# A fused FFT mixing and MoE kernel: the scheduler's order replaced by one from a list scheduler with measured lengths

## The chip, the cores and the metric

The kernel runs on one core of a Trainium2 chip. Its time is the device time of one execution in microseconds (us). Five engines each work through a queue of their own in order: TensorE (PE, with its weight loads shown as PEld), VectorE (DVE), ScalarE (ACT), GpSimd (POOL) and SyncE (SP), which only issues DMAs. They meet at semaphores: an instruction waits at the head of its queue until what it reads is written and what it overwrites has been read.

## The reference

Eight sequences of 3136 positions and 256 channels go through a real FFT along the positions, a complex 256 x 256 mixing, a soft threshold, the inverse FFT, and then one SoLU feed-forward layer for each of the 25088 tokens:

```python
X = np.fft.rfft(x, axis=1)                       # x: (8, 3136, 256)
Yr = Xr @ w_r - Xi @ w_i + b_r;  Yi = Xr @ w_i + Xi @ w_r + b_i
Y = sign(Y) * max(abs(Y) - 0.01, 0)              # on Yr and Yi
y = np.fft.irfft(Yr + 1j * Yi, n=3136, axis=1)
h = y.reshape(25088, 256) @ w_in                 # (25088, 1024)
solu = h * softmax(h)
ln = (solu - mean(solu)) / sqrt(var(solu) + 1e-6) * g_ln
out = ln @ w_out                                 # (25088, 256)
```

## The kernel before

Nearly all matmuls are in fp16 with every operand split into a high and a low half, so a product takes three matmuls (high by high, high by low, low by high).

**Front, for each of the 8 batches b.** The FFT of 3136 = 98 x 32 goes in two steps. `load_peak` (L190) loads x in 8 pieces and takes their largest value; `set_scales` (L200) makes powers of two of it. `fwd1` (L238) loads x again in 8 chunks, splits it (xh, xl), multiplies by the 98-point matrix (L254) and writes s1 to DRAM; batch 0 uses `fwd1_first` in f32 (L261) and takes its peaks on the way. `fwd2` (L313) is the 32-point step in 13 units (12 of two frequencies, one of one): it loads `bin` from s1, multiplies (L337) and splits into Xh and Xl. `mix` (L395, with L385, for batch 0 L363) is the complex mixing and the threshold. `inv1` (L416, L438) is the inverse 32-point step, in two halves of PE's rows, and writes s2 to DRAM. `inv2` (L462, L473) loads `zt` from s2 in 8 groups, does the inverse 98-point step, and writes 392 tokens at a time, transposed, to a ring of 1024 tokens (`ring_hi`, `ring_lo`).

**Feed-forward, for each of 196 tiles of 128 tokens.** `moe_head` (L493): 2 x 6 matmuls of 512 columns (L504) into PSUM tiles `ph` (3 buffers), the row's maximum (L507), a handful of one-column operations, the exponential (L524) and its product with h (L525) into `u` (4 buffers). `moe_turn` (L536): u split into `lh` (L540, ScalarE) and `ll` (L542, GpSimd), each transposed by a DMA of SyncE (L545) into `th` and `tl` (3 buffers each), and the variance (L549 to L553). `moe_tail` (L556): 24 matmuls of 256 columns (L563) into the one buffer of `po`, the scaled copy (L566) and the stores (L574). Weights come as 64-bit floats and are turned into f32 on VectorE and GpSimd by `load_wide` (L148).

**What sets the order.** The program is written in an order by hand: front units of batch b + 1, with the loads and fwd1 of batch b + 2 beside them, are handed out between the tiles of batch b by shares of their estimated cost (`front_b`, `with_shares`, `advance`, L724 to L758). A head is followed by its turn two tiles later, and that by its tail two tiles later; inv2 runs up to two tiles ahead of need (L780). The framework's scheduler then sets each engine's order, going by this program order and by a simulation of the engines' times (`schedule_with_timeline_sim=True`, L817). A few loads are held back by a tiny GpSimd copy into their buffer that reads an earlier load (L153, L180, L196):

```python
nc.gpsimd.tensor_copy(t[:1, 0, 0, :1], before)
nc.sync.dma_start(t, src)
```

Of the kernel before, what the change touches and what calls it, by code (L numbers as in the profile page):

```python
# [94 lines left out]

@with_exitstack
def fft_mix_solu_kernel(ctx: ExitStack, tc, x, w_r, w_i, b_r, b_i, w_in, w_out, g_ln, fa, fa16, fb, fs, gb, gs, ia, out):
    nc = tc.nc
    B, _, D = x.shape
    FF = w_in.shape[1]  # L100
    P = 128
# [8 lines left out]
    const = ctx.enter_context(tc.tile_pool(name="const", bufs=1))  # L110
    dram = ctx.enter_context(tc.tile_pool(name="dram", bufs=2, space=DRAM))
    xp = ctx.enter_context(tc.tile_pool(name="xp", bufs=2))
    fp = ctx.enter_context(tc.tile_pool(name="fp", bufs=2))
    mp = ctx.enter_context(tc.tile_pool(name="mp", bufs=2))
    sp = ctx.enter_context(tc.tile_pool(name="sp", bufs=4))
    ps_h = ctx.enter_context(tc.tile_pool(name="ps_h", bufs=3, space=PSUM))
    ps_o = ctx.enter_context(tc.tile_pool(name="ps_o", bufs=1, space=PSUM))
    ps_f = ctx.enter_context(tc.tile_pool(name="ps_f", bufs=4, space=PSUM))
# [25 lines left out]
    make_identity(nc, ident)  # L144
# [3 lines left out]
    def load_wide(dst, src, before=None):  # L148
# [3 lines left out]
        if before is not None:  # L152
            nc.gpsimd.tensor_copy(raw[:1, :1].bitcast(F32), before)  # L153
# [24 lines left out]
    def load_after(t, src, before):  # L178

        nc.gpsimd.tensor_copy(t[:1, 0, 0, :1], before)  # L180
        nc.sync.dma_start(t, src)
# [8 lines left out]
    def load_peak(b, c):  # L190

        n = S * D // P // NPK
        t = xp.tile([P, C1], F32, name="xt", bufs=3)[:, :n]
        if b == 1 and c < 3:

            nc.gpsimd.tensor_copy(t[:1, :1], raw[0, 4][:1, 0, :1])  # L196
        nc.sync.dma_start(t, x[b].rearrange("s d -> (s d)").rearrange("(p c n) -> c p n", p=P, c=NPK)[c])
        note_peak(b, c, NPK, t)
# [39 lines left out]
    def fwd1(b, c):  # L238
# [11 lines left out]
        for h in range(C1 // HF):  # L250
            hs = slice(h * HF, (h + 1) * HF)
            pa = front_psum(b)
            for i, (t, j) in enumerate(((xh, 0), (xh, 1), (xl, 0))):
                nc.tensor.matmul(pa[:N1], fa16_s[:, j], t[:, hs], start=i == 0, stop=i == 2)  # L254
# [6 lines left out]
    def fwd1_first(c):  # L261
# [9 lines left out]
        for h in range(C1 // HF):  # L271
            hs = slice(h * HF, (h + 1) * HF)
            pa = front_psum(0)
            nc.tensor.matmul(pa[:N1], fa_s, xt[:, hs], start=True, stop=True)
            nc.scalar.copy(av[:, hs], pa[:N1])
# [9 lines left out]
    def load_bin(b, g):  # L285
# [8 lines left out]
        nc.sync.dma_start(t, v[:, g * QG : (g + 1) * QG])  # L294
        raw[b, g] = t
        load_after(gb_s[g].rearrange("p u r t m -> p u (r t) m"), gb[:, g * QG // 2 : (g + 1) * QG // 2].rearrange("p u r t m -> p u (r t) m"), t[:1, 0, :1])
        if g + 1 < Q // QG:
            load_after(fb_s[g + 1], fb[:, (g + 1) * QG : (g + 2) * QG], t[:1, 0, :1])
# [14 lines left out]
    def fwd2(b, u):  # L313
# [11 lines left out]
        else:  # L325
# [3 lines left out]
            bt, fw = bins[b, g], [fb_s[g][:, gi + i] for i in range(2)]  # L329

        pb = front_psum(b)
        pv = pb.rearrange("p (r h i c) -> p r h i c", r=2, h=ND, i=2)
        for i in range(n):
            for dh in range(ND):
                ds = slice(dh * P, (dh + 1) * P)
                for k, (t, j) in enumerate(((0, 0), (0, 1), (1, 0))):
                    nc.tensor.matmul(pv[:, :, dh, i], bt[:, gi + i, t, ds], fw[i][:, j], start=k == 0, stop=k == 2)  # L337

        xh = fp.tile([P, 3, ND, 2, 2 * N2], F16, name="Xh16", bufs=2)
        xl = fp.tile([P, 3, ND, 2, 2 * N2], F16, name="Xl", bufs=2)  # L340
        if b:
            xs = fp.tile([P, ND, 2, 2 * N2], F32, name="Xs", bufs=1)
            nc.scalar.activation(xs[:, :, :n], pv[:, 1, :, :n], AF.Copy, scale=B_SCALE)
# [9 lines left out]
    def mix_first(u):  # L353
# [3 lines left out]
        xh, xl = Xs.pop((0, u))  # L357
        pm = front_psum(0)
        k = 0
        for part in (1, 0):  # L360
            for dh in range(ND):
                for x, w in ((xh, w_hi), (xh, w_lo), (xl, w_hi)):
                    nc.tensor.matmul(  # L363
                        pm[:M], x[:, part, dh, :n], w[dh][:, 1 - part : 3 - part], start=k == 0, stop=k == 6 * ND - 1
                    )
                    k += 1
        t = fp.tile([P, 2, D], F32, name="yt")
# [5 lines left out]
    def mix_split(b, u):  # L373
# [6 lines left out]
        ps, pm = front_psum(b), front_psum(b)  # L380
        for part, wp, out in ((2, 1, ps[:M, :D]), (1, 4, pm[:M, :D]), (0, 3, pm[:M, D:])):
            k = 0
            for dh in range(ND):
                for x, w in ((xh, w_hi), (xh, w_lo), (xl, w_hi)):
                    nc.tensor.matmul(out, x[:, part, dh, :n], w[dh][:, wp], start=k == 0, stop=k == 3 * ND - 1)  # L385
                    k += 1
        t = fp.tile([P, 2, D], F32, name="yt")
# [28 lines left out]
    def inv1(b, u0, u1):  # L416
# [14 lines left out]
        for u in range(u0, u1):  # L431
            yh, yl = Ys.pop((b, u))
            for k, (t, j) in enumerate(((yh, 0), (yl, 0), (yh, 1))):
                for ri in range(2):
                    for i in range(n):
                        rows = slice(i * half, (i + 1) * half)
                        gw = gs_s[:, ri, j] if n == 1 else gb_s[g][rows, u % 2, ri, j]
                        nc.tensor.matmul(  # L438
                            pz[i][:K, (u - u0) * D : (u - u0 + 1) * D], gw, t[rows, ri], start=k + ri == 0, stop=k + ri == 3
                        )  # L440
# [21 lines left out]
    def inv2(b, g):  # L462
# [5 lines left out]
        for eh in range(ND):  # L468
            pa = ps_f.tile([P, HF], F32, name="pf")
            for i in range(G2):  # L470
                es = slice(eh * P, (eh + 1) * P)
                for k, (t, j) in enumerate(((0, 0), (0, 1), (1, 2))):
                    nc.tensor.matmul(pa[:, i * N1 : (i + 1) * N1], zt[:, i, t, es], ia_s[:, j], start=k == 0, stop=k == 2)  # L473
# [19 lines left out]
    def moe_head(k, spare):  # L493
# [4 lines left out]
        for h in range(2):  # L498
# [3 lines left out]
            for dh in range(ND):  # L502
                for lh, rh in ((hi, win_hi), (hi, win_lo), (lo, win_low)):
                    nc.tensor.matmul(p, lh[:, dh], rh[:, dh, cs], start=n == 0, stop=n == 3 * ND - 1)  # L504
                    n += 1
# [50 lines left out]
    def moe_tail(k, parts, r, spare=False):  # L556
# [3 lines left out]
        for part, halves in ((th, 2), (tl, 1)):  # L560
            for f in range(NF):
                for j in range(halves):
                    nc.tensor.matmul(po[:, :D], part[:, f], wout[:, f, j], start=n == 0, stop=n == 3 * NF - 1)  # L563
                    n += 1
# [15 lines left out]
    for k in range(12):  # L580
        nc.tensor.matmul(pw[:, :P], ones, ones, start=k == 0, stop=k == 11)
    for c in range(NCH):
        fwd1_first(c)

# [13 lines left out]
    for j in range(2 * ND):  # L598
        nc.tensor.matmul(pw[:, :D], ones, wa[:, j], start=j == 0, stop=j == 2 * ND - 1)
# [87 lines left out]
    def moe_w_out():  # L687
# [4 lines left out]
        for f in range(0, NF, 2):  # L692
            load_wide(wo_s[f // 2], w_out[f * P : (f + 2) * P].rearrange("(f p) e -> p f e", p=P), raw[0, 3][:1, 0, :1])
# [5 lines left out]
    def finish_w_out(wo_s):  # L699
# [13 lines left out]
        for j in range(2):  # L713
            nc.tensor.matmul(pw[:, :D], ones, total[:, j], start=j == 0, stop=j == 1)
# [9 lines left out]
    def front_a(b):  # L724

        return [(0.1, load_peak, (b, c)) for c in range(NPK)] + [(0.1, set_scales, (b,))] + [(1.45, fwd1, (b, c)) for c in range(NCH)]

    def front_b(b, beside=()):


        units, beside = [], list(beside)
        lag = 4 if b == 0 else 3
        for step in range(NU + lag):
            for cost, fn, u in ((0.73, fwd2, step), (2.2, mix, step - 1)):
                if 0 <= u < NU:
                    units.append((cost, fn, (b, u)))
            n = -(-len(beside) // (NU - step)) if step < NU else 0
            units += beside[:n]
            del beside[:n]
            u = step - lag  # L740
            if u == NU - 1 or 0 <= u < NU and b == 0:

                units.append((0.87, inv1, (b, u, u + 1)))
            elif 0 < u < NU and u % 2:
                units.append((1.74, inv1, (b, u - 1, u + 1)))
        units.append((4, None, ()))
        return units

    def advance(units, share):

        while units and units[0][3] <= share + 1e-6:
            _, fn, args, _ = units.pop(0)
            if fn is not None:
                fn(*args)

    def with_shares(units):
        ends = np.cumsum([u[0] for u in units]) if units else []
        return [(*u, e / ends[-1]) for u, e in zip(units, ends)]  # L758

    moe_w_in(0)  # L760
    set_scales(0)
    for _, fn, args in front_b(0):
        if fn is not None:
            fn(*args)
    moe_w_in(1, raw[0, 0][:1, 0, :1])
    finish_w_in()
    set_h_scale(0)
    later_mix_weights()
    finish_w_out(moe_w_out())
    heads, turned = [], []  # L770
    for b in range(B):
        tiles = range(0, 24) if b % 2 == 0 else range(24, 49)
        units = front_b(b + 1, front_a(b + 2) if b + 2 < B else ()) if b + 1 < B else []
        if b == 0:
            units = front_a(1) + units
        units = with_shares(units)
# [44 lines left out]
```

## Time and profile before

| what | us |
|---|---|
| median of 3 runs | 1749.53 (1748.41 to 1754.09) |
| the profiled execution | 1751.33 |
| its span, first to last instruction | 1749.5 |
| busy: PE / DVE / ACT / POOL | 1622.8 / 1406.9 / 1251.2 / 1142.8 |
| mean granted TensorE clock | 0.972 |

A group's row in the profile has the line, engine, operation, what it writes <- reads, the count, then its busy time and mean length in ns, then the idle time of the engine just before it and what ended that. PE's busy time counts pipelined matmuls with modelled ends, so the distance between starts says more about its pace. A row of waits has who waited, for whom, the total in us, the number of waits and the longest. A row of the chain or timeline has the start, the length, the engine and what ran.

### The profile page before, as it was taken

What the parts mean: (1) busy time and instruction counts of PE and PEld (TensorE: products, weight loads), DVE (VectorE), ACT (ScalarE), POOL (GpSimd) and SP (SyncE); (2) the same over time, 40 slices, a digit from 0 to 9 for tenths busy, and PEclk for the clock granted to TensorE, in tenths of its full rate; (3) what the DMA queues carried; (4) which work ended last, traced back from release to release, by engine and by line L of the source; (5) the groups of instructions that cost most, each with busy time, mean ns of one, the idle gap of its engine ahead of it and who ended that gap; (6) DMA issues with size and microseconds to landing.
All of it is one profiled execution on the core that took longest, in us unless ns stands there. A gap on an engine that the chain in (4) does not pass through costs nothing.

```text
span 1749.5 us, 38321 instructions
## 1 busy us (share of the span) xinstructions
PE 1622.8 (93%) x13220; PEld 1131.6 (65%) x13220; DVE 1406.9 (80%) x3399; ACT 1251.2 (72%) x2511; POOL 1142.8 (65%) x1909
## 2 busy tenths in 40 slices
PE   5777799999989999899999999999999989999998
PEld 3434476667766767567666676666767667766765
DVE  5887698879887798868889798887998767876764
ACT  4566577667857777667777777677787767776776
POOL 1654376668746776558766786666776757775665
PEclk8888899999989999999999999999999999999999
DMA  7736978787877868767897877869686765657866
GB/s 248 234 106 157 242 149 189 184 182 150 182 202 155 159 153 193 181 166 142 167 189 173 175 145 190 175 173 198 138 183 142 153 155 116 143 112 161 138 123 113
DMA packets 531268, 290.25 MB, mean 166 GB/s; under 512 B 425758, under 2 KB 502016, under 8 KB 531072
## 3 DMA queue, kind: packets, MB, share of 16 engines
q1 hardware_dynamic: 531072, 287.80, 73.5%
q8 instruction: 103, 1.69, 0.4%
q14 instruction: 93, 0.76, 0.1%
HBM read 107.88 MB, written 77.07 MB: 106 GB/s over the span
## 4 chain that ended last, share of the span: by engine, by line
PE 52%; DVE 19%; DMA 11%; ACT 7%; issue 6%; POOL 4%; SPq 0%; DVEq 0%; ACTq 0%; POOLq 0%
PE ph L504 19%; PE po L563 18%; PE pf L385 6%; DMA xt<-in_x_dram 4%; DVE u L525 3%; PE pf L473 3%; DVE nm L507 2%; DMA th<-lh 2%; PE pf L438 2%; DVE xl L247 2%; PE pf L337 2%; PE pf L254 2%; ACT lh L540 2%; DVE peaks L188 1%; POOL ll L542 1%
## 5 line engine op out<-in xcount | busy, mean ns | idle before, releaser
L542 POOL TENSOR_TENSOR ll<-u,lh 128x1024 f16<-128x1024 f32 x196 | 422.5, 2156 | 148.7 <-ACT lh L540 144.0
L563 PE MATMUL po<-wout,th 128*128 128x256 f16 x3104 | 390.6, 276 | 20.0 <-DMA th<-lh 15.2
L524 ACT ACTIVATE u<-ph,m,hsb 128x512 f32<-128x512 f32 x384 | 295.4, 775 | 138.0 <-DVE m L511 137.3
L507 DVE TENSOR_REDUCE nm<-ph 128x1 f32<-128x512 f32 x390 | 266.5, 686 | 128.3 <-PE ph L504 124.1
L563 PEld LDWEIGHTS <-th 128*128 128x128 f16 x3136 | 305.5, 99 | 97.8 <-DMA th<-lh 22.7
L504 PE MATMUL ph<-win_hi,ring_hi 128*128 128x512 f16 x780 | 300.2, 385 | 17.5 <-DVE u L525 16.9
L504 PE MATMUL ph<-win_lo,ring_hi 128*128 128x512 f16 x780 | 299.4, 384 | 0.0
L504 PE MATMUL ph<-win_low,ring_lo 128*128 128x512 f16 x780 | 297.1, 383 | 0.0
L525 DVE SCALAR_TENSOR_TENSOR u<-ph,ch,u 128x512 f32<-128x512 f32 x390 | 278.7, 748 | 18.5 <-ACT u L524 1.8
L540 ACT CAST lh<-u 128x1024 f16<-128x1024 f32 x196 | 205.3, 1048 | 83.9 <-DVE u L525 81.8
L504 PEld LDWEIGHTS <-ring_hi 128*128 128x128 f16 x1568 | 149.5, 99 | 153.9 <-issue 32.3
L549 ACT ACTIVATE junk<-u,total 128x1024 bf16<-128x1024 f32 x196 | 225.6, 1151 | 5.8 <-POOL total L529 5.8
L563 PE MATMUL po<-wout,tl 128*128 128x256 f16 x1552 | 207.9, 273 | 8.2 <-DMA tl<-ll 8.1
L563 PEld LDWEIGHTS <-tl 128*128 128x128 f16 x1568 | 152.5, 98 | 38.1 <-DMA tl<-ll 11.5
L385 PE MATMUL pf<-w_hi,Xh 128*128 128x256 f16 (+1 forms) x546 | 149.6, 274 | 6.3 <-DVE av L258 5.0
L409 POOL TENSOR_TENSOR y<-yt,yc 128x512 f32<-128x512 f32 (+1 forms) x104 | 134.9, 1297 | 26.5 <-DVE yc L408 12.3
L385 PE MATMUL pf<-w_lo,Xh 128*128 128x256 f16 (+1 forms) x546 | 149.6, 274 | 0.0
L385 PE MATMUL pf<-w_hi,Xl 128*128 128x256 f16 (+1 forms) x546 | 149.4, 274 | 0.0
L530 POOL TENSOR_TENSOR se<-se,se 128x1 f32<-128x1 f32 x196 | 37.6, 192 | 153.1 <-ACT u L524 127.3
L504 PEld LDWEIGHTS <-ring_lo 128*128 128x128 f16 x784 | 77.2, 99 | 93.2 <-issue 4.6
L566 ACT ACTIVATE o<-po,r 128x256 f32<-128x256 f32 x194 | 91.8, 473 | 60.6 <-PE po L563 50.7
L413 POOL TENSOR_TENSOR yl<-y,yh 128x512 f16<-128x512 f32 (+1 forms) x104 | 121.7, 1170 | 18.6 <-ACT yh L412 17.2
(220 smaller groups left out, 3106.4 us busy)
## 6 DMA issues: line engine op xcount, KB each, us to landing
xt<-in_x_dram SPq DMA_DIRECT2D x112, 392.0 KB
zt<-s SPq DMA_DIRECT2D x64, 392.0 KB
s<-av SPq DMA_DIRECT2D x56, 392.0 KB
bin<-s SPq DMA_DIRECT2D x42, 512.0 KB
s<-zout SPq DMA_DIRECT2D x42, 512.0 KB
out_dram<-o SPq DMA_DIRECT2D x64, 98.0 KB
u<-in_x_dram SPq DMA_DIRECT2D x8, 392.0 KB
th<-lh SPq DMA_TRANSPOSE x196
```

What stands on the lines that cost most here:

```text
L385: nc.tensor.matmul(out, x[:, part, dh, :n], w[dh][:, wp], start=k == 0, stop=k == 3 * ND - 1)
L409: nc.gpsimd.tensor_sub(y[:M], t[:M], c[:M])
L413: nc.gpsimd.tensor_sub(yl[:M], y[:M], yh[:M])
L504: nc.tensor.matmul(p, lh[:, dh], rh[:, dh, cs], start=n == 0, stop=n == 3 * ND - 1)
L507: nc.vector.tensor_reduce(m, p, AX.X, ALU.max, negate=True)
L524: nc.scalar.activation(u[:, cs], ph[h], AF.Exp, bias=m, scale=down, accum_out=se[h])
L525: nc.vector.scalar_tensor_tensor(u[:, cs], ph[h], ch, u[:, cs], ALU.mult, ALU.mult, accum_out=su[h])
L540: nc.scalar.copy(hi, u)
L542: nc.gpsimd.tensor_sub(lo, u, hi)
L549: nc.scalar.activation(junk, u, AF.Square, bias=total, scale=-float(FF), accum_out=var)
L563: nc.tensor.matmul(po[:, :D], part[:, f], wout[:, f, j], start=n == 0, stop=n == 3 * NF - 1)
L566: nc.scalar.activation(o, po[:, :D], AF.Copy, scale=r)
```

## The change

The computation, the tiles, the buffers and nearly every instruction stay. `nc` becomes a `Plan`: calls such as `nc.vector.tensor_reduce(...)` are no longer issued but written down as operations (`Op`), with the tiles they touch, what they depend on, a key, and a length from a formula. At the end `nc.issue(tc)` orders all of them by list scheduling and issues them in that order, which the framework is told to keep (`manual_schedule`). At each step the planner takes, for each engine, the operations that can start first, of these the one with the lowest key, and of the engines' candidates the one that starts first. Buffers count: an operation that opens a new tile can't start before a buffer is free; SBUF tiles of one name are opened in the order of their keys, PSUM tiles in any.

- Matmuls that fill one PSUM tile form one operation (`together`); a tail is two, one for th and one for tl.
- `reserve` makes a matmul group start, in the plan, only when the tiles that its result will go to are free as well.
- `hold` takes the place of the tiny GpSimd copies: in the plan the load starts after the earlier load has landed; on the chip it is only issued behind it.
- Keys are tile numbers: head n has n, its turn n + 0.5, its tail n + 1; inv2 has n - 2 for the tile that needs it, and only the groups that this tile needs are asked for; the front's units are spread evenly over the tiles; batch 0's front has -130 to -70, w_in -128 to -64, w_out -30 and -0.5, batch 1's loads and fwd1 0 to 5.
- The extra PSUM buffer of the last tails goes to the last tile alone.

```diff
+    CALL = dict(vector=58.0, scalar=52.0, gpsimd=110.0)
+    ELEMENT = dict(vector=1.07, scalar=0.83, gpsimd=2.03)
+    SCALAR = dict(vector=60.0, scalar=92.0, gpsimd=140.0)
+    SEEN = dict(tensor=250.0, vector=160.0, scalar=190.0, gpsimd=160.0, sync=90.0)
...
+        if name == "dma_start":
+            cross = kw.get("transpose", False)
+            op.length += 1500.0 if cross else 430.0
+            op.moved += 1500.0 if cross else size / 270.0
+        elif op.engine == "tensor":
+            n = moving.cells.size * (4 if moving.dtype == F32 else 1) * 0.42 + 1
+            op.half = "gb" in ins[0].tile.kw["name"]
+            op.length += n / 2 if op.half else n
+        else:
+            op.length += self.CALL[op.engine] + big * self.ELEMENT[op.engine] + max(scalars, 0) * self.SCALAR[op.engine]
...
+            for e in self.ENGINES:
+                can = [(may_start(op), op) for op in ready[e]]
+                first = min(at for at, _ in can)
+                _, _, at, op = min((op.key, op.seq, at, op) for at, op in can if at <= first + 1.0)
+                if best is None or at < best[0]:
+                    best = at, op
...
+            op.end = free[e] = at + op.length
+            if op.moved:
+                bus = max(bus, op.end) + op.moved
+                op.end = bus + 2000.0
...
-            nc.gpsimd.tensor_copy(raw[:1, :1].bitcast(F32), before)
+            nc.hold(before)
...
-            while groups < N2 // G2 and groups * G2 * N1 < need + 2 * P:
+            while groups < N2 // G2 and groups * G2 * N1 < need:
+                nc.key = first + n - 2
                 inv2(b, groups)
                 groups += 1
 
+            nc.key = first + n
             heads.append(moe_head((b // 2, t), b == B - 1 and n == 0))
-            if len(heads) > 2:
-                turned.append(moe_turn(*heads.pop(0)))
-            advance(units, (n + 0.5) / len(tiles))
-            if len(turned) > 2:
-                moe_tail(*turned.pop(0))
-            advance(units, (n + 1) / len(tiles))
+            nc.key = first + n + 0.5
+            turned.append(moe_turn(*heads.pop(0)))
+            nc.key = first + n + 1
+            moe_tail(*turned.pop(0), b == B - 1 and n > L - 3 and n % 2 == 0)
...
+    nc.issue(tc)
```

More of the change, by code (lines that the diff above doesn't have):

```diff
@@ L1 @@
+import re
+from bisect import insort
 from contextlib import ExitStack
@@ new lines, in _rearrange @@
+def _rearrange(a, pattern, sizes):
+    sides = [[p.strip("()").split() for p in re.findall(r"\([^)]*\)|\w+", s)] for s in pattern.split("->")]
+    sizes = {**sizes, sides[0][0][0]: 1}
+    for group, n in zip(sides[0], a.shape):
+        unknown = [k for k in group if k not in sizes]
+        known = int(np.prod([sizes[k] for k in group if k in sizes]))
+        if unknown:
+            sizes[unknown[0]] = n // known
+    names = [k for g in sides[0] for k in g]
+    a = a.reshape([sizes[k] for k in names]).transpose([names.index(k) for g in sides[1] for k in g])
+    return a.reshape([int(np.prod([sizes[k] for k in g])) for g in sides[1]])
@@ L252, in fwd1 @@
             pa = front_psum(b)
-            for i, (t, j) in enumerate(((xh, 0), (xh, 1), (xl, 0))):
-                nc.tensor.matmul(pa[:N1], fa16_s[:, j], t[:, hs], start=i == 0, stop=i == 2)
+            nc.reserve(av[:, h * HF // D : (h + 1) * HF // D])
+            with nc.together():
+                for i, (t, j) in enumerate(((xh, 0), (xh, 1), (xl, 0))):
+                    nc.tensor.matmul(pa[:N1], fa16_s[:, j], t[:, hs], start=i == 0, stop=i == 2)
             pv = pa[:N1].rearrange("p (n d) -> p n d", d=D)
@@ L329, in fwd2 @@
             bt, fw = bins[b, g], [fb_s[g][:, gi + i] for i in range(2)]
+        xh = fp.tile([P, 3, ND, 2, 2 * N2], F16, name="Xh16", bufs=2)
+        xl = fp.tile([P, 3, ND, 2, 2 * N2], F16, name="Xl", bufs=2)
+        xs = fp.tile([P, ND, 2, 2 * N2], F32, name="Xs", bufs=1) if b else None
+        nc.reserve(xh, xl, *([xs] if b else []))
         pb = front_psum(b)
         pv = pb.rearrange("p (r h i c) -> p r h i c", r=2, h=ND, i=2)
[L333 to L340, printed above, removed]
+        with nc.together():
+            for i in range(n):
+                for dh in range(ND):
+                    ds = slice(dh * P, (dh + 1) * P)
+                    for k, (t, j) in enumerate(((0, 0), (0, 1), (1, 0))):
+                        nc.tensor.matmul(pv[:, :, dh, i], bt[:, gi + i, t, ds], fw[i][:, j], start=k == 0, stop=k == 2)
         if b:
-            xs = fp.tile([P, ND, 2, 2 * N2], F32, name="Xs", bufs=1)
             nc.scalar.activation(xs[:, :, :n], pv[:, 1, :, :n], AF.Copy, scale=B_SCALE)
@@ L357, in mix_first @@
         xh, xl = Xs.pop((0, u))
+        t = fp.tile([P, 2, D], F32, name="yt")
+        nc.reserve(t)
         pm = front_psum(0)
         k = 0
[L360 to L367, printed above, removed]
+        with nc.together():
+            for part in (1, 0):
+                for dh in range(ND):
+                    for x, w in ((xh, w_hi), (xh, w_lo), (xl, w_hi)):
+                        nc.tensor.matmul(
+                            pm[:M], x[:, part, dh, :n], w[dh][:, 1 - part : 3 - part], start=k == 0, stop=k == 6 * ND - 1
+                        )
+                        k += 1
         nc.vector.scalar_tensor_tensor(
@@ L380, in mix_split @@
         ps, pm = front_psum(b), front_psum(b)
+        t = fp.tile([P, 2, D], F32, name="yt")
+        nc.reserve(t)
         for part, wp, out in ((2, 1, ps[:M, :D]), (1, 4, pm[:M, :D]), (0, 3, pm[:M, D:])):
             k = 0
[L383 to L387, printed above, removed]
+            with nc.together():
+                for dh in range(ND):
+                    for x, w in ((xh, w_hi), (xh, w_lo), (xl, w_hi)):
+                        nc.tensor.matmul(out, x[:, part, dh, :n], w[dh][:, wp], start=k == 0, stop=k == 3 * ND - 1)
+                        k += 1
         un = scales[b]["mix"][:M]
@@ L430, in inv1 @@
         pz = [front_psum(b) for _ in range(n)]
[L431 to L440, printed above, removed]
+        nc.reserve(zo[:, gi : gi + n * w])
+        with nc.together():
+            for u in range(u0, u1):
+                yh, yl = Ys.pop((b, u))
+                for k, (t, j) in enumerate(((yh, 0), (yl, 0), (yh, 1))):
+                    for ri in range(2):
+                        for i in range(n):
+                            rows = slice(i * half, (i + 1) * half)
+                            gw = gs_s[:, ri, j] if n == 1 else gb_s[g][rows, u % 2, ri, j]
+                            nc.tensor.matmul(
+                                pz[i][:K, (u - u0) * D : (u - u0 + 1) * D], gw, t[rows, ri], start=k + ri == 0, stop=k + ri == 3
+                            )
         m = n * w
@@ L469, in inv2 @@
             pa = ps_f.tile([P, HF], F32, name="pf")
[L470 to L473, printed above, removed]
+            nc.reserve(*(ring[:, eh, to : to + z - a] for ring in (ring_hi, ring_lo) for a, z, to in ((0, first, j0), (first, n, 0)) if z > a))
+            with nc.together():
+                for i in range(G2):
+                    es = slice(eh * P, (eh + 1) * P)
+                    for k, (t, j) in enumerate(((0, 0), (0, 1), (1, 2))):
+                        nc.tensor.matmul(pa[:, i * N1 : (i + 1) * N1], zt[:, i, t, es], ia_s[:, j], start=k == 0, stop=k == 2)
             for a, z, to in ((0, first, j0), (first, n, 0)):
@@ L501, in moe_head @@
             n = 0
[L502 to L505, printed above, removed]
+            with nc.together():
+                for dh in range(ND):
+                    for lh, rh in ((hi, win_hi), (hi, win_lo), (lo, win_low)):
+                        nc.tensor.matmul(p, lh[:, dh], rh[:, dh, cs], start=n == 0, stop=n == 3 * ND - 1)
+                        n += 1
             m = sp.tile([P, 1], F32, name="nm")
@@ L560, in moe_tail @@
         for part, halves in ((th, 2), (tl, 1)):
[L561 to L564, printed above, removed]
+            with nc.together():
+                for f in range(NF):
+                    for j in range(halves):
+                        nc.tensor.matmul(po[:, :D], part[:, f], wout[:, f, j], start=n == 0, stop=n == 3 * NF - 1)
+                        n += 1
         o = mp.tile([P, D], F32, name="o", bufs=2)
@@ L579, in fft_mix_solu_kernel @@
     pw = ps_o.tile([P, HF], F32, name="po")
-    for k in range(12):
-        nc.tensor.matmul(pw[:, :P], ones, ones, start=k == 0, stop=k == 11)
+    with nc.together():
+        for k in range(12):
+            nc.tensor.matmul(pw[:, :P], ones, ones, start=k == 0, stop=k == 11)
+    nc.key = -200
     for c in range(NCH):
         fwd1_first(c)
+    nc.key = -190
     def wide_tile():
@@ L597, in fft_mix_solu_kernel @@
     pw = front_psum(0)
-    for j in range(2 * ND):
-        nc.tensor.matmul(pw[:, :D], ones, wa[:, j], start=j == 0, stop=j == 2 * ND - 1)
+    with nc.together():
+        for j in range(2 * ND):
+            nc.tensor.matmul(pw[:, :D], ones, wa[:, j], start=j == 0, stop=j == 2 * ND - 1)
     gain = const.tile([P, 1], F32, name="gain")
@@ L712, in finish_w_out @@
         pw = ps_f.tile([P, HF], F32, name="pf")
-        for j in range(2):
-            nc.tensor.matmul(pw[:, :D], ones, total[:, j], start=j == 0, stop=j == 1)
+        with nc.together():
+            for j in range(2):
+                nc.tensor.matmul(pw[:, :D], ones, total[:, j], start=j == 0, stop=j == 1)
         cm = mp.tile([P, D], F32, name="o", bufs=2)
@@ L722, in finish_w_out, with front_a @@
             nc.gpsimd.tensor_sub(wout[:, fs, 1], half, wout[:, fs, 0])
[L724 to L731, printed above, removed]
+    def front_a(b, key, step):
+        for fn, args in [(load_peak, (b, c)) for c in range(NPK)] + [(set_scales, (b,))] + [(fwd1, (b, c)) for c in range(NCH)]:
+            nc.key = key
+            fn(*args)
+            key += step
@@ L732, in front_b @@
+    def front_b(b, key, step):
         lag = 4 if b == 0 else 3
-        for step in range(NU + lag):
-            for cost, fn, u in ((0.73, fwd2, step), (2.2, mix, step - 1)):
+        for n in range(NU + lag):
+            nc.key = key + n * step
+            for fn, u in ((fwd2, n), (mix, n - 1)):
                 if 0 <= u < NU:
[L736 to L740, printed above, removed]
+                    fn(b, u)
+            u = n - lag
@@ L741, in front_b @@
             if u == NU - 1 or 0 <= u < NU and b == 0:
-                units.append((0.87, inv1, (b, u, u + 1)))
+                inv1(b, u, u + 1)
             elif 0 < u < NU and u % 2:
[L745 to L758, printed above, removed]
@@ L760, in fft_mix_solu_kernel @@
-    moe_w_in(0)
[L761 to L765, printed above, removed]
+                inv1(b, u - 1, u + 1)
+    nc.key = -140
+    set_scales(0)
+    front_b(0, -130, 4)
+    nc.key = -128
+    moe_w_in(0)
+    nc.key = -120
+    moe_w_in(1, raw[0, 0])
+    nc.key = -64
     finish_w_in()
     set_h_scale(0)
+    nc.key = -30
+    wo_s = moe_w_out()
+    nc.key = -0.5
+    finish_w_out(wo_s)
     later_mix_weights()
-    finish_w_out(moe_w_out())
@@ L770, in fft_mix_solu_kernel @@
     heads, turned = [], []
+    first = 0
     for b in range(B):
         tiles = range(0, 24) if b % 2 == 0 else range(24, 49)
-        units = front_b(b + 1, front_a(b + 2) if b + 2 < B else ()) if b + 1 < B else []
+        L = len(tiles)
         if b == 0:
-            units = front_a(1) + units
-        units = with_shares(units)
+            front_a(1, 0, 0.3)
+        if b + 2 < B:
+            front_a(b + 2, first + 6, (L - 6) / 17)
+        if b + 1 < B:
+            front_b(b + 1, first + (6 if b == 0 else 0), (L - (8 if b == 0 else 2)) / (NU + 3))
@@ L793, in fft_mix_solu_kernel @@
             groups += 1
-    turned += [moe_turn(*head) for head in heads]
-    for n, parts in enumerate(turned):
-        moe_tail(*parts, n % 2 == 0)
+        first += L
+    nc.issue(tc)
 _INS = ["x", "w_r", "w_i", "b_r", "b_i", "moe_w_in", "moe_w_out", "moe_g_ln"]
```

244 lines of the change are left out of this document (226 added, 18 removed).

## The prediction

> **What bounds the kernel now.** I read the page's totals first, then the busy time by stage, then the list of who waited for whom, and last the timeline of single microseconds for the pitch of each operation.
>
> ```profile
> span 1749.5 us, 38321 instructions
> PE 1622.8 (93%) x13220; PEld 1131.6 (65%) x13220; DVE 1406.9 (80%) x3399; ACT 1251.2 (72%) x2511; POOL 1142.8 (65%) x1909
> ...
> 0.00:131.00 131.00, 92.06 (x533) 49.53 (x533) 100.06 (x192) 71.81 (x134) 58.03 (x64) 0.87 0.61 196
> 131.00:218.00 87.00, 63.14 (x389) 37.67 (x390) 63.40 (x146) 52.49 (x97) 36.02 (x60) 0.85 0.81 198
> 218.00:1224.00 1006.00, 959.05 (x8048) 681.90 (x8046) 851.25 (x2025) 737.89 (x1492) 682.47 (x1132) 0.99 0.78 173
> 1224.00:1399.00 175.00, 173.00 (x1460) 122.70 (x1459) 151.24 (x368) 137.27 (x276) 129.62 (x214) 1.00 0.71 154
> 1706.00:1749.00 43.00, 36.28 (x272) 26.06 (x270) 20.59 (x64) 26.39 (x53) 25.73 (x52) 0.99 0.67 114
> ```
>
> The columns of the stages are: length, busy time of PE, PEld, DVE, ACT and POOL, granted clock, DMA share, GB/s. TensorE (PE) is the fullest engine everywhere. Two stages stand out: up to 131 us and from there to 218 us PE is busy for only seven tenths, at a granted clock of 0.87 and 0.85; later it is 0.98 to 1.00. The stage from 1224 to 1399 us is the best that this kernel shows.
>
> A busy PE isn't a PE at its peak, so I count its work by the distance from one matmul's start to the next.
>
> ```profile
> 1708.97 2.59 PE ph L504 x12
> 1711.56 2.62 PE po L563 x24
> 1605.65 2.16 PE pf L473 x48
> ...
> 805.59 0.27 PE L385 MATMUL pf<-w_lo,Xh 128*128 128x256 f16 x1
> 805.70 0.27 PE L385 MATMUL pf<-w_hi,Xl 128*128 128x256 f16 x1
> 807.45 0.55 PE L337 MATMUL pf<-fb,bin 128*128 128x128 f16 x7
> 839.28 0.60 PE L438 MATMUL pf<-yh,gb 64*128 64x256 f16 x8
> 9.34 1.02 PE L274 MATMUL ph<-u,fa_s 98*98 98x512 f32 x2
> 10.20 1.02 PE L274 MATMUL pf<-u,fa_s 98*98 98x512 f32 x2
> ```
>
> That is 0.216 us for 512 columns (2.59/12), 0.109 for 256, 0.045 for 98, about 0.056 for 128, 0.43 for the f32 ones; the 64-row pairs of inv1 run side by side, a pair in 0.109 (four pairs in 0.60, with 0.27 for the last). The 196 token tiles cost 2.59 + 2.62 = 5.21 us each, 1021 us. Each of the seven later batches has fwd1 48 x 0.216 = 10.4, fwd2 150 x 0.056 = 8.4, mix 234 x 0.109 = 25.5, inv1 78 x 0.109 = 8.5 and inv2 192 x 0.045 = 8.6, together 61.4, so 430 us. Batch 0 has 32 x 0.43 = 13.8 for fwd1, 156 x 0.216 = 33.7 for mix, and the same fwd2, inv1 and inv2: 73. With warm-up and scales, 8 us, the sum is 1532 us of the 1749.5. The other 217 us are what an order can win. They lie as follows.
>
> Up to 131 us the work is that of batch 0 without inv2 and the warm-up, 72 us, so 59 are lost. From 131 to 218 us:
>
> ```profile
> L504 PE MATMUL ph<-win_hi,ring_hi 128*128 128x512 f16 x34 | 14.9, 437 | 6.6 <-DVE u L525 6.4
> L563 PE MATMUL po<-wout,th 128*128 128x256 f16 x96 | 14.7, 317 | 9.4 <-DMA th<-lh 9.2 <-ACT o L566 0.3
> L254 PE MATMUL pf<-xh,fa_s 98*98 98x512 f16 x32 | 9.7, 391 | 0.1
> L563 PE MATMUL po<-wout,tl 128*128 128x256 f16 x44 | 6.6, 276 | 3.2 <-DMA tl<-ll 3.1
> L254 PE MATMUL pf<-xl,fa_s 98*98 98x512 f16 x16 | 5.9, 379 | 0.0
> L473 PE MATMUL pf<-ia_s,zt 98*128 98x98 f16 x72 | 4.8, 232 | 6.9 <-DMA zt<-s 6.9
> ```
>
> With three such groups of L504 (102 x 0.216 = 22), 140 x 0.109 = 15.3, 48 x 0.216 = 10.4, 72 x 0.045 = 3.2 and 1.3 for the first fwd2, this stage does 52 us of work in 87: 35 lost, and 19.2 of them are waits for DMA (9.2 + 3.1 + 6.9). The rest of the run, 1531.5 us, then holds 1532 - 72 - 52 = 1408 us of work: 123 lost. The stage from 1224 to 1399, counted in the same way by its grouped lines, has 169 us of work in 175, so its loss is 3.2%. At that pace the rest would take 1408/0.968 = 1455, plus some 15 us for the last tile's chain, 1470: 61 us less than it does.
>
> Over the whole run these waits stand against loads and transposes:
>
> ```profile
> DVE peaks L188 <- DMA xt<-in_x_dram: 28.7, 26, 2.9
> PEld L563 <- DMA th<-lh: 22.7, 14, 7.3
> PE pf L473 <- DMA zt<-s: 17.9, 6, 6.9
> PE ph L504 <- DVE u L525: 16.9, 18, 4.1
> PE po L563 <- DMA th<-lh: 15.2, 8, 6.4
> PE po L563 <- DMA tl<-ll: 8.1, 5, 3.1
> ```
>
> **The change part by part.** No operation of the five engines changes but some twenty tiny GpSimd copies, which go. The lever is the order alone. It can only be as good as its lengths, so I held these against the trace.
>
> ```profile
> 805.30 0.75 DVE L525 SCALAR_TENSOR_TENSOR u<-ph,ch,u 128x512 f32<-128x512 f32 x1
> 805.98 0.75 DVE L525 SCALAR_TENSOR_TENSOR u<-ph,ch,u 128x512 f32<-128x512 f32 x1
> 803.13 0.78 ACT L524 ACTIVATE u<-ph,m,hsb 128x512 f32<-128x512 f32 x1 [0.28 <-DVE m L511]
> 803.90 0.77 ACT L524 ACTIVATE u<-ph,m,hsb 128x512 f32<-128x512 f32 x1
> 808.04 2.13 POOL L542 TENSOR_TENSOR ll<-u,lh 128x1024 f16<-128x1024 f32 x1
> 807.84 1.24 SPq L545 DMA_TRANSPOSE th<-lh  x1
> q1 hardware_dynamic: 531072, 287.80, 73.5%
> xt<-in_x_dram SPq DMA_DIRECT2D x112, 392.0 KB
> ...
> 1741.50 3.13 DMA tl<-ll
> 195.49 8.78 DMA th<-lh
> 373.84 6.93 DMA th<-lh
> ```
>
> The plan gives L525 58 + 512 x 1.07 + 60 = 666 ns (pitch in the trace 680), L524 52 + 425 + 184 + 92 = 753 (770), L542 110 + 2079 = 2189 (2130), a 512-column matmul 216 (216), a transpose 1.5 us on the queue (1.24). Its bus takes 392 transposes x 1.5, and for the other 185 MB (287.8 less 392 x 0.262) 270 GB/s, 1273 us; the queue's row has 73.5% of 1749.5 = 1286. So its lengths are the pitches of this chip. Its one latency for landing, 1.5 + 1.5 + 2.0 = 5.0 us for a transpose on an idle bus, lies between the 3.1 of the drained end and the 8.8 of the crowded start.
>
> Steady part (after 218 us). Tail units now come on PE when the plan has their transposes landed, in two groups (th, tl) that other work may part; front units of the next batches get keys spread over the tiles, where now two of the side units (loads for peaks, fwd1) ride on each early step. The bounds are 0, if the present order loses nothing by choice, and the 61 us of the best stage's pace; a loss is the second rival's. I take three quarters, 45: the losses named by rows, 17.9 + 15.2 + 8.1 of PE waiting for DMA and 28.7 of VectorE, are of the kind the plan's bus foresees, and the quarter stays for landings that scatter.
>
> Stage from 131 to 218. The 48 matmuls of fwd1 of batch 1 and their 16 loads of 392 KB (112 for seven batches, peaks among them) stand in it now, because their units are handed out with the tiles. With key 0 and an engine never left idle while anything can start, they may run in the gaps before 131 us, where PE is idle for 131 - 92 = 39 us. The bounds are 0 (VectorE, busy 100 of 131, has no room) and 35. I take 22: the 10.4 us of fwd1 and 12 of the 19.2 us of DMA waits, as fewer loads meet the first transposes.
>
> Stage up to 131. VectorE, with 100 us of 131, is its bound, since all weights pass it. The keys put the second half of w_in and w_out behind the units of batch 0; the copies on GpSimd that waited for loads go, and the order on the SP queue alone takes their place, so a weight load can come earlier and meet a load that matters. From -10 (such a meeting costs one or two landings, 5 to 9 us by the rows above) to +20 (half of the 31 us VectorE is idle, and what that frees behind it); I take 10, the nearer to the first tile's weights that move back.
>
> `reserve` and the grouped matmuls cost nothing on the chip: they only choose the order, and a pair of inv1 is never parted. Fewer inv2 groups ahead (need without two tiles) take away slack: the chain of inv1's write, zt's load and inv2 must fit two tiles, some 16 us, and costs 6.9 us, the longest zt wait, at each of seven batch ends if it doesn't; I leave that to the quarter above. The last tile's chain stays.
>
> The sum is 45 + 22 + 10 = 77. The profiled execution took 1751.3 us, 1.8 more than its span and than the median 1749.5; against the median it is 1749.5 - 77 = 1672.5, so 1673.
>
> By the Trainium skill (TensorE: Matmul & The Clock Gate, Part 1: The HAM clock gate), an idle window of about 3.4 us halves the matmul clock. The trace agrees: 0.85 in the stage with the 6.9 us wait for zt, 1.00 in the one from 1224 us. Were the second stage's gaps all closed, the rule would give 63 x 0.15 = 9 us more, 1664; were they only moved, nothing; I count nothing apart.
>
> **The rivals.** First, that it hardly reorders. The present order is itself the outcome of a scheduler that simulates the engines, and PE is at 93%. If it already fills what can be filled, only the moved fwd1 counts, 10 us: 1740. Against it speak the 28.7 and 41 us of waits for loads, that such a simulation should have hidden.
>
> Second, slower: late tails. Each engine issues in the plan's order, so a transpose that lands after its planned 5 us stops PE with every head behind it; now heads are taken two tiles ahead of the turn and that two ahead of the tail. If one tile in three has the 8.8 us of the crowded row, 3.8 late, that is 196/3 x 3.8 = 248 us before slack; with a third of it not caught up by buffers, 83, and the gain is gone: 1755, with half not caught up, 1797. It decides at 77/196 = 0.39 us per tile. For it speak landings of 6.9 and 8.8; against it that PE, fullest of all, has a queue of ready work, so tails will mostly stand landed. The skill's same page (Architectural detail) says that ScalarE's and VectorE's queues are strictly in order: a late instruction holds all behind it, as the 22.7 us row of L563 shows on PE.
>
> Third, that all of it is won: 61 + 35 + 20 = 116, 1633.
>
> **How the numbers follow.** The forecast (1650 to 1710 its own range) has 0.57, all won 0.15, hardly reordered 0.15, late tails 0.13. A difference under 0.3%, 5 us, is about what a measurement of this kernel can't tell from none. Of the second, about half would lie within it: faster 0.80, same 0.07, slower 0.13. The range from 1625 to 1748 leaves out the late tails and a few hundredths below, and reaches to the others.
>
> **What would show it.** PE's matmuls unchanged in number, the clock in the second stage above 0.95, L254 of batch 1 ahead of the first L504, L504 starting before 130 us, PE's waits for th, tl and zt under half of now, peaks' wait for xt near nothing. Wrong would be: waits of L563 for th above 80 us in total, VectorE above 92% with PE waiting for it, or loads ahead of the transposes on the SP queue, with 0.9 and more of DMA share over whole stages.

## The result and the profile after

The changed kernel takes 1735.09 us (median of 7) against 1750.26; the ratio is 0.991 (0.9883 to 0.9936). It is 15 us faster, clear of the noise, and that is a fifth of the 77 us that were forecast. First the page's totals and the same stages as before, with the same columns; every line of the program now bears the number of the planner's helper, so groups are told by their tiles.

```profile
span 1737.6 us, 38336 instructions
PE 1606.1 (92%) x13220; PEld 1123.6 (65%) x13220; DVE 1432.0 (82%) x3399; ACT 1251.4 (72%) x2511; POOL 1146.1 (66%) x1889
...
0.00:131.00 131.00, 89.99 (x533) 48.40 (x533) 102.51 (x185) 69.46 (x132) 50.67 (x44) 0.83 0.56 179
131.00:218.00 87.00, 75.25 (x534) 48.09 (x535) 80.38 (x194) 67.46 (x128) 51.01 (x88) 0.95 0.96 232
218.00:1224.00 1006.00, 947.46 (x8031) 675.74 (x8030) 858.15 (x2012) 735.04 (x1483) 685.65 (x1117) 0.98 0.79 173
1224.00:1399.00 175.00, 167.34 (x1398) 118.86 (x1398) 146.56 (x342) 130.46 (x259) 123.46 (x200) 0.99 0.73 151
1399.00:1706.00 307.00, 302.60 (x2561) 216.68 (x2560) 230.28 (x627) 229.68 (x474) 216.64 (x406) 1.00 0.73 139
```

Up to 131 us nothing is won. From 131 to 218 us PE is busy for 75 us instead of 63 and at 0.95 of its clock. After 218 us nothing is won, and the formerly best stretch, 1224 to 1399, now does less. VectorE is busy for 25 us more, with the same operations. The second stage by its groups, and then who PE waited for over the whole run:

```profile
L312 PE MATMUL ph<-win_hi,ring_hi 128*128 128x512 f16 x48 | 19.1, 399 | 10.7 <-DVE u L312 10.7
L312 PE MATMUL po<-wout,th 128*128 128x256 f16 x131 | 15.8, 273 | 0.2 <-DMA th<-lh 0.2
L312 PE MATMUL pf<-xh,fa_s 98*98 98x512 f16 x32 | 9.5, 379 | 0.0
L312 PE MATMUL pf<-ia_s,zt 98*128 98x98 f16 x144 | 9.4, 232 | 0.9 <-DMA zt<-s 0.9
L312 PE MATMUL po<-wout,tl 128*128 128x256 f16 x64 | 8.3, 272 | 0.0
L312 PE MATMUL pf<-xl,fa_s 98*98 98x512 f16 x16 | 6.1, 378 | 0.0
```

```profile
PE ph L312 <- DVE u L312: 40.8, 37, 2.9
PE po L312 <- DMA th<-lh: 11.8, 12, 2.6
PE ph L312 <- ACT av L312: 8.3, 1, 8.3
PE pf L312 <- DMA fa_s<-in_fa_dram: 8.0, 1, 8.0
PE pf L312 <- DVE Xl L312: 6.7, 6, 1.8
PE pf L312 <- DMA zt<-s: 5.3, 3, 2.3
PE po L312 <- DMA tl<-ll: 2.7, 5, 1.0
```

Counted as in the prediction (three groups of L504 with 48 matmuls each, of which the first is shown), that stage does 144 x 0.216 + 195 x 0.109 + 48 x 0.216 + 144 x 0.045 = 69 us, 17 more than before; the whole span is 12 shorter, so the rest lost some 5. PE's waits for th, tl and zt fell from 41 to 20 us, as the plan's bus promised. What replaced them is the first row: PE waits for VectorE's u, which holds the PSUM tiles of the next head, 40.8 us against 16.9.

Why VectorE is late is seen in a timeline (start, length, engine, what ran), where PE's matmul carries the wait before it in brackets:

```profile
1221.00 2.45 DVE L312 TENSOR_SCALAR yc<-yt,sc 128x512 f32<-128x512 f32 x1
1221.04 2.13 POOL L312 TENSOR_TENSOR ll<-u,lh 128x1024 f16<-128x1024 f32 x1 [0.67 <-DMA tl<-ll]
...
1223.37 0.20 DVE L312 TENSOR_SCALAR ch<-c,hsb 128x1 f32<-128x1 f32 x1
1223.67 0.75 DVE L312 SCALAR_TENSOR_TENSOR u<-ph,ch,u 128x512 f32<-128x512 f32 x1
1224.35 0.75 DVE L312 SCALAR_TENSOR_TENSOR u<-ph,ch,u 128x512 f32<-128x512 f32 x1
1224.48 0.38 PE L312 MATMUL ph<-win_hi,ring_hi 128*128 128x512 f16 x1 [1.57 <-DVE u L312]
```

The clip yc, which takes 0.55 us by itself, takes 2.45 beside GpSimd's ll (recorded as starting 0.04 us behind it) and ends 0.28 us after ll; ch and u come behind it in VectorE's queue, and PE behind u. By tile, with min/median/max in ns, before and after, and then the group rows of both kernels with their means:

```profile
L408 DVE TENSOR_SCALAR yc<-yt,sc x91: 524/546/2453, 222.2 to 1572.7; 128x512 f32<-128x512 f32 x84, 64x512 f32<-64x512 f32 x7
L312 DVE TENSOR_SCALAR yc<-yt,sc x91: 529/673/2448, 231.7 to 1547.2; 128x512 f32<-128x512 f32 x84, 64x512 f32<-64x512 f32 x7
...
L408 DVE TENSOR_SCALAR yc<-yt,sc 128x512 f32<-128x512 f32 x84 | 72.7, 865 | 0.9
L247 DVE SCALAR_TENSOR_TENSOR xl<-xt,sc,xh 98x1024 f16<-98x1024 f32 x56 | 79.3, 1424 | 9.7 <-ACT xh L246 8.6 <-DMA out_dram<-o 0.9
L312 DVE TENSOR_SCALAR yc<-yt,sc 128x512 f32<-128x512 f32 x84 | 83.1, 990 | 1.4
L312 DVE SCALAR_TENSOR_TENSOR xl<-xt,sc,xh 98x1024 f16<-98x1024 f32 x56 | 92.1, 1646 | 2.5 <-ACT xh L312 2.3
```

The plan gives yc 726 ns and xl 1214. The trace bears the collision out for all of them: of the 91 clips, the eight with no GpSimd operation beside them take 530 to 546 ns, and every longer one overlaps one; of the 56 xl, the four without take 1269 to 1276, and the mean of the others is 1674. The u operation, which takes one of its inputs from PSUM, never takes more than 753. The Trainium skill (SBUF — State Buffer, SBUF: two separate sides) describes it: VectorE and GpSimd share a pair of SBUF ports under an exclusive lock, taken by GpSimd's operations and by VectorE's that have two SBUF inputs or run in a two-port mode. The trace agrees in that xl has two SBUF inputs and is stretched, and that the 2.45 us is ll's 2.13 and a little; that yc runs in a two-port mode can't be read from it, only that yc is stopped when it reads SBUF and not when it reads PSUM (e2).

The plan also tells how it should have gone: by the planner's own count the changed kernel ends at 1656 us, and the chip's span is 1737.6. The plan starts the first head at 123 us, the chip at 136; 15 us more are lost between tiles 14 and 21, and then on average two or three in every seven tiles up to tile 147. In the last two batches (from some 1400 us) nothing more is lost: there are no loads for peaks, no xl and at the end no yc, and VectorE, 230 us of 307, has room. That fits the collisions, but doesn't prove them to be the loss: the experiments have to.

### The profile page after: what moved, and what is told of

Its sections match the earlier page's. It is cut to its first block, busy times and chain, and to the rows that moved or that the text cites. A ratio compares the mean times of both kernels' runs of the same rounds, so it can differ in the third digit from the quotient of the medians.

```text
span 1737.6 us, 38336 instructions
## 1 busy us (share of the span) xinstructions
PE 1606.1 (92%) x13220; PEld 1123.6 (65%) x13220; DVE 1432.0 (82%) x3399; ACT 1251.4 (72%) x2511; POOL 1146.1 (66%) x1889
## 4 chain that ended last, share of the span: by engine, by line
PE 57%; DVE 19%; DMA 7%; issue 6%; ACT 6%; POOL 5%; SPq 0%; DVEq 0%; ACTq 0%; POOLq 0%
PE po L312 20%; PE ph L312 20%; PE pf L312 17%; DVE u L312 4%; DMA th<-lh 2%; DVE nm L312 2%; DMA tl<-ll 2%; DVE xl L312 2%; POOL ll L312 2%; ACT u L312 2%; DVE av L312 1%; DVE yt L312 1%; ACT lh L312 1%; ACT junk L312 1%; POOL y L312 1%
## 5 line engine op out<-in xcount | busy, mean ns | idle before, releaser
L312 POOL TENSOR_TENSOR ll<-u,lh 128x1024 f16<-128x1024 f32 x196 | 430.2, 2195 | 134.8 <-ACT lh L312 128.9
L312 PE MATMUL po<-wout,th 128*128 128x256 f16 x3120 | 377.5, 275 | 14.2 <-DMA th<-lh 11.8
L312 PE MATMUL ph<-win_hi,ring_hi 128*128 128x512 f16 x780 | 299.3, 384 | 41.1 <-DVE u L312 40.8
L312 ACT ACTIVATE junk<-u,total 128x1024 bf16<-128x1024 f32 x196 | 225.5, 1150 | 14.5 <-POOL total L312 14.4
L312 PE MATMUL po<-wout,tl 128*128 128x256 f16 x1560 | 202.4, 273 | 2.7 <-DMA tl<-ll 2.7
L312 PE MATMUL pf<-w_hi,Xl 128*128 128x256 f16 (+2 forms) x550 | 150.4, 273 | 3.0 <-DVE Xl L312 3.0
L312 PE MATMUL pf<-w_hi,Xh 128*128 128x256 f16 (+2 forms) x550 | 150.7, 274 | 1.2 <-ACT Xh L312 0.9
L312 POOL TENSOR_TENSOR yl<-y,yh 128x512 f16<-128x512 f32 (+1 forms) x104 | 126.5, 1216 | 36.3 <-ACT yh L312 35.1
L312 PE MATMUL pf<-w_lo,Xh 128*128 128x256 f16 (+2 forms) x550 | 150.3, 273 | 0.0
L312 PEld LDWEIGHTS <-Xh 128*128 128x128 f16 (+1 forms) x1196 | 114.2, 99 | 31.4 <-issue 6.2
```

The costliest lines, as they stand in the source:

```text
L312: getattr(engine, name)(*args, **kw)
```

## The experiments

Theory A: the plan doesn't know of that shared port. Theory B: DMAs land later than planned. In all runs but e8 the planner makes its order anew from what the edit tells it. Times below are medians; ratios go to the kernel before in the same session.

**e1, the port in the plan.**

```diff
+                if len(sbuf) > 1 or name == "tensor_scalar" and wide and len(sbuf) == len(wide):
+                    op.port = True        # VectorE; GpSimd's operations all have it
...
+            if op.port:
+                at = max(at, held[other[op.engine]])
```

> Theory A (port): the plan lost its gain because it does not know that a VectorE operation with both inputs in SBUF, or a wide tensor_scalar on SBUF, and a GpSimd operation shut each other out. Here the planner alone is changed: such an operation may not start while the other engine's one is planned to run. Its own plan ends at 1666 us instead of 1656. A expects 1695 to 1710 us, VectorE's busy time down by 40 us or more from 1432, the mean of yc near 0.6 us instead of 0.99. Theory B (landings): the DMAs land later than planned and tails hold up PE; the port is noise. B expects 1730 to 1745 us.

1712.14 us, 0.9791 (0.9772 to 0.9809). VectorE's busy time is 1385.7 us, 46 less; the wait of PE for u goes from 40.8 to 31.2 and the mean of yc to 0.72:

```profile
L318 DVE TENSOR_SCALAR yc<-yt,sc 128x512 f32<-128x512 f32 x84 | 60.2, 717 | 0.8
L318 DVE SCALAR_TENSOR_TENSOR xl<-xt,sc,xh 98x1024 f16<-98x1024 f32 x56 | 81.3, 1452 | 0.8 <-ACT xh L318 0.8
```

A expected 1710 at the most; it is 2 us over, with yc at 0.72 where A said near 0.6, and B's range is missed by 18.

**e2, the clip from PSUM.** `nc.vector.tensor_scalar(c[:M], pm[:M]..., up, down, ALU.min, ALU.max)` in place of `t[:M]`.

> As the changed kernel, but the soft threshold's clip yc (84 + 7 operations) reads the product in PSUM instead of yt in SBUF, so it needs no second SBUF port; bias and the other product are left out of the clip. A expects yc at a steady 0.65 to 0.75 us instead of 0.55 to 2.4, and about 12 us less, 1723. B expects no change, 1730 to 1740.

1721.68 us, 0.9846 (0.9829 to 0.9864): 13 less, as A said, though the clip is longer than A's 0.65 to 0.75:

```profile
L312 DVE TENSOR_SCALAR yc<-pf,sc x91: 779/801/812, 226.6 to 1531.4; 128x512 f32<-128x512 f32 x84, 64x512 f32<-64x512 f32 x7
...
PE ph L312 <- DVE u L312: 46.2, 41, 2.9
```

All 91 clips now take 0.80 us (at most 0.81), the 83 beside a GpSimd operation like the 8 without: for the operation, that shows the lock. The 13 us aren't the lock's alone. The clip no longer needs yt, so the planner makes another order: counted by operation and tile, 1565 of VectorE's 3399 instructions are at the place in its queue that they had in the changed kernel. And PE waits longer for u than there, 46.2 us against 40.8, so the gain didn't come through that wait.

**e8, the same edit in the kernel before.**

> The kernel before with the clip yc reading the product in PSUM, as in the run of the changed kernel that gained 13 us by it. If the port costs the order before as much, 1737 or less; if it costs mainly the planned order, 1745 to 1750: its yc takes 0.87 us on average against 0.99.

0.997 (0.9951 to 0.9989), 1744.34 us: some 5 us, just under the range that was expected if the lock costs mainly the planned order. The old order meets the lock less: its yc takes 865 ns on average against 990, as the rows above show. Here, too, the edit changes the order as well.

**e3 and e6, later landings**, `op.end = bus + 3000.0` and `4000.0`.

> As the changed kernel, but the planner lets every DMA land 3.0 us after the bus instead of 2.0; its plan ends at 1661 us. B expects the waits of PE for th, tl and zt, 20 us, to go down by two thirds and the time to 1715 to 1722. A expects no more than 5 us either way.

> As the changed kernel, but the planner lets every DMA land 4.0 us after the bus instead of 2.0 (3.0 gave 1713); its plan ends at 1666 us. Theory B (landings are late) expects a further 5 to 10 us, 1704 to 1709, if landings spread beyond 6 us; if 3.0 covers them, the longer plan shows, 1715 to 1722. Theory A alone expects 1735 to 1745.

1713.46 us, 0.9802 (0.9781 to 0.9823), and 1715.92, 0.9805 (0.9789 to 0.9821). For 3.0 the time is within 2 us of B's range, and A's "no more than 5" fell; PE's waits for th, tl and zt went from 20 to 5.5, as B said (th alone from 11.8 to 3.8). Nothing more comes at 4.0.

**e9 and e10, halves of that.**

> As the changed kernel, but only the transposes land 3.0 us after the bus in the plan, loads and stores 2.0 as before; its plan ends at 1651 us. In the run with 3.0 for all, 22 us were won. If the late ones are the transposes (PE's waits for th and tl, 15 us), all of it comes: 1710 to 1716. If they are the loads (zt, bin, xt), nothing: 1730 to 1736.

> The other half: loads and stores 3.0 us, the transposes 2.0; the plan ends at 1666 us. The mirror of the run before it: 1730 to 1745 if the transposes are the late ones, 1710 to 1720 if the loads are.

0.9799 (0.9776 to 0.9822) and 0.9815 (0.9792 to 0.9837). Neither is the mirror of the other: each half wins what the whole did. With the loads alone later, PE waits for th as long as ever (12.7 us), and yet the time falls. B in its simple form, that the gain is the late landings' own waits, is false, too.

**e4, fa_s first** (`nc.key = -210` around its load).

> As the changed kernel, but the load of the 98-point matrix fa_s has the lowest key and is issued first; in the changed kernel PE waits 8.0 us for it. If that wait is on the path, 4 to 8 us less; both A and B allow that, neither explains more.

0.9891 (0.9873 to 0.991): about 4 us, with an interval that overlaps that of the changed kernel (0.9883 to 0.9936), so not shown by the times. VectorE, ScalarE and GpSimd run the same order as in the changed kernel, and the first head starts 6 us earlier, at 130.

**e5, a control.**

> A control: the changed kernel with VectorE's planned time of one element 1.071 ns instead of 1.07, which means nothing on the chip but shuffles the order; its plan ends at 1657 us like the changed kernel's. It tells how much of a difference is luck of the order: within 6 us of 1735 if the earlier gains of 22 us are gains of their causes; 1715 or less would make them luck.

1736.3 us, 0.9911 (0.9898 to 0.9924). This shuffle wins nothing, but it is a small one: 3099 of VectorE's 3399 instructions keep their place in its queue. In the eight other edits without the port (e3, e6, e9 to e11, e13 to e15) it is 742 to 1306, in e1 1109. That a larger reshuffle alone wins something is a rival that this control doesn't exclude.

**e11, longer lengths in place of the port.**

> As the changed kernel, but in place of the port the plan only gets longer lengths for the two operations that the port delays most, to the means that the changed kernel's trace shows: yc + 264 ns, xl + 432 ns. The plan ends at 1668 us. If the gain of the port's edit (23 us) comes from not putting the two operations side by side, yc and xl keep their means and the time stays at 1725 to 1735. If a plan with true mean lengths is enough, 1710 to 1716.

0.9804 (0.9783 to 0.9824): as good as the port, though yc still takes 0.87 and xl 1.61 us on average. So a gain of 20 us needs no separation, and e1 by itself doesn't show what the port costs.

**e13 and e14, slack where nothing was too short**: ScalarE's element 0.92, every result seen 60 ns later.

> As the changed kernel, but a length is taken away from what the trace bears out: ScalarE's element 0.92 ns instead of 0.83, 8% more in all. The plan still ends at 1657 us. If the gains of 20 us come from correcting what the plan had too short, nothing: 1730 to 1740. If any pessimism that loosens the order wins as much, 1710 to 1720.

> As the changed kernel, but every engine's result is seen 60 ns later by the others in the plan. The plan ends at 1666 us. Slack of a general kind, spread over every dependence. General slack theory: 1705 to 1720; correction theory: 1728 to 1740.

0.9848 (0.9822 to 0.9874), between the two theories' ranges, and 0.9815 (0.9789 to 0.984), in the range of general slack: 11 and 17 us, with nothing corrected. One reading is that the order was too tight, so that any slack helps. The other is that rival of e5: the changed kernel's order is a poor one of its kind, and any order far enough from it is better. No run parts the two.

**e7, port, landings at 3.0 and fa_s together, and e15, the same with longer lengths in place of the port.**

> The three edits of the planner together: the port, landings at 3.0 us, fa_s first. Its plan ends at 1663 us. If port and landings are separate losses of 23 and 22 us, they add up with the 5 of fa_s: 1680 to 1690. If both only give PE's order slack, either of them does it and the two together give 1705 to 1712.

> Landings at 3.0 us and fa_s first, with the longer lengths of yc and xl in place of the port; the plan ends at 1660 us. With the port these three gave a ratio of 0.9621 to the kernel before. If the mean lengths do what the port's edit does, 0.960 to 0.966, 1680 to 1692; if keeping the two operations apart is worth something by itself, 0.967 to 0.975, 1693 to 1707.

1685.38 us, 0.9621 (0.9609 to 0.9634), against 0.9788 (0.9763 to 0.9813). e15 is above both its ranges, where landings (0.9802) and longer lengths (0.9804) were alone: the two add nothing to each other. The port does add to the landings, and e7 is in the range for separate losses. VectorE's rows and PE's waits tell them apart, e7's and then e15's, where the two collide more than ever:

```profile
L318 DVE TENSOR_SCALAR yc<-yt,sc 128x512 f32<-128x512 f32 x84 | 58.3, 695 | 0.8
L314 DVE TENSOR_SCALAR yc<-yt,sc 128x512 f32<-128x512 f32 x84 | 93.6, 1114 | 1.2
...
PE ph L318 <- DVE u L318: 24.4, 28, 2.0
PE ph L314 <- DVE u L314: 37.3, 33, 3.4
```

VectorE's busy time is 1381.8 us in e7 and 1444.7 in e15. So keeping the two engines apart is worth some 28 us where the landings have slack. That is more than a reshuffle gives: the eight edits without the port, in eight widely different orders, all lie between 0.979 and 0.985. What lies between them and the changed kernel's 0.991, 11 us or more, is a second loss, whose cause is open as said under e14.

**e16, port and the 60 ns, without the landings.**

> The port and fa_s first, and in place of later landings every engine's result is seen 60 ns later; the plan ends at 1688 us, 25 more than with the landings. If any slack does beside the port what the landings did, 0.960 to 0.970, 1680 to 1697. If it was the landings themselves, the plan's 25 us and the late DMAs both show: 0.973 to 0.982, 1702 to 1718.

0.970 (0.9664 to 0.9737), on the border of the first range: other slack beside the port does part of what the landings did, at a longer plan. That leaves open how much of it is landings.

**e12, also the half clock, and e17, that with the 60 ns.** The plan doubles the lengths of matmuls for a while after PE was idle:

```diff
+                if at - free[e] > 2500.0:
+                    cold = at + 3400.0
+                if at < cold:
+                    op.length *= 2
```

> The three edits together, and the planner also doubles the length of matmuls for 3.4 us after each idle time of PE over 2.5 us and for the first 4 us. Its plan ends at 1660 us, against 1663. The drift of the chip against the plan in the run without it was 25 us, of which little lies before the first tile. If the half clock is what is left, 1670 to 1678; if not, 1682 to 1690.

> Port, landings at 3.0, fa_s, the half clock, and the 60 ns too; the plan ends at 1690 us, against 1660 without the 60 ns (which gave a ratio of 0.9577). If the slack is used up by then, the longer plan shows and the ratio is 0.963 or more; if more slack still wins, 0.957 or less.

0.9577 (0.9558 to 0.9596), 1679.13 us, 1 us over the range for the half clock: the best kernel of this study, 4.2% under the one before, with no change of what is computed. Against its plan's end, 1660, the chip's span is 17 us longer. With the 60 ns it is 0.969 (0.9662 to 0.9718): more slack now costs about what the longer plan does.

```profile
131.00:218.00 87.00, 77.56 (x563) 49.76 (x561) 77.18 (x191) 69.14 (x134) 49.36 (x94) 0.94 0.92 215
218.00:1650.00 1432.00, 1397.06 (x11980) 1006.02 (x11979) 1189.43 (x2979) 1092.59 (x2214) 1023.56 (x1724) 1.00 0.79 169
```

These are e12's stages: after 218 us the clock is 1.00 and PE is busy for 97.6%.

## Why the prediction was right or wrong

**Steady part, forecast 45, measured a loss of some 5: the step that failed.** It is the sentence "So its lengths are the pitches of this chip". I held the plan against five operations, each in one undisturbed moment, and none of them was one that GpSimd can stop. The group row of before, yc with a mean of 865 against a median of 546 and a maximum of 2453, contradicted the sentence, and I didn't quote it. What the runs put in its place: yc and xl, planned at 726 and 1214 ns, take 990 and 1646 on average in the changed kernel, some 46 us more on VectorE than planned (84 x 0.264 + 56 x 0.432). With the port, the landings and fa_s in the plan, 50 us come back in e7 (0.991 to 0.9621); 28 of them go with the port (e7 against e15), fa_s may have a few, and for the rest it is open whether slack or only another order does it. That e12 comes within 6 us of the sum's 1673 is in part luck: it also has the half clock in the plan, for which the prediction counted nothing, and its first head still starts at 136 us.

**The plan's bus** was right in its direct effect: the waits for th, tl and zt halved, 41 to 20, and DVE's wait for xt no longer shows among the long ones. It was wrong to book that as time: PE's wait for u grew from 16.9 to 40.8 us, 24 more where the others gave back 21. I had quoted the row of u, 16.9, and asked nothing of it. Nor is that wait a measure of the loss by itself: e2, e3 and e9 have 46.2, 42.6 and 44.9 us of it and are, by their ratios, 11 to 19 us faster than the changed kernel.

**Stage from 131 to 218: 22 forecast, 17 measured**, but for half the reason. The DMA waits went (19.2 to 1.1, in part for 10.7 on u); fwd1 of batch 1 did not move ahead, its 48 matmuls still stand there, and the DMA share is 0.96, where 0.9 and more was part of a sign of being wrong. In e7 it does move ahead, from 130.7 us with the first head at 144.2. The clock is 0.95, where "above 0.95" was to show the step right; for its rise from 0.85 the sum counted nothing.

**Up to 131: 10 forecast, 0 measured.** The first head starts at 136 us against 138. fa_s got key 0, behind x's loads of key -200, and PE waits 8.0 us for it; e4 moved it, and its first head starts at 130.

**The rivals.** The number that came is that of "hardly reorders", 1740, but not its reason: the order changed throughout, and its gain was lost. That it came so near is luck. "Late tails" named the right kind of thing, a plan too early with a strict queue behind it, on the wrong engine: tails held PE for 14.5 us in all, far under 77, and the longest wait of PE was for VectorE. The sign that was named for VectorE, above 92% with PE waiting for it, was set too high: it is at 82%.

## What to carry to other kernels

Before trusting the lengths of a planner, compare mean, median and maximum of each group, and where they differ, look for what ran beside the long ones. Model a lock as a resource, not only as a longer length (0.9621 against 0.9788 with the rest alike). Some slack may help and more may cost (e12 against e17). A new order changes everything at once: before a gain of 1 or 2% is put down to its cause, compare it with several orders that differ as widely for no reason. A planner's own end is a forecast that can be held against the chip tile by tile, which shows where the difference grows.

## What the runs showed of the hardware that I had not expected

A VectorE operation that reads PSUM in place of SBUF can be the steadier one though it is slower by itself: the clip from PSUM takes 0.80 us each time, whatever GpSimd does, against 0.55 at best and 0.99 on average from SBUF. The kernel with it is 13 us shorter, in an order that changed as well. And with the same 13220 matmuls, PE's busy time is 1606 us in the changed kernel at a mean granted clock of 0.974, and 1586 in e7 at 0.980; how much of the difference is the clock's, no run shows.
